# A written order for four engines in the opening of a three-stage kernel: gram copies first, weight conversions spread over more steps

## The chip, the cores and the metric

One Trainium2 chip, one of its cores. The metric is the device time of one execution in microseconds (us), the median of three runs. Engines are called by their short names: PE is TensorE, DVE is VectorE, ACT is ScalarE, POOL is GpSimd, SP is SyncE (here it only issues DMAs). PSUM is the memory that PE writes; SBUF is the working memory.

## The reference, cut to what matters

Three stages follow each other: a delta-rule attention, a dense MLP and a top-1 mixture of experts. Only the first two overlap with the change.

```python
def _attn_ref(q, k, v, beta):            # (4, 8, 768, 48) each, beta (4, 8, 768)
    k_n = k / (np.linalg.norm(k, axis=-1, keepdims=True) + 1e-06)
    state = np.zeros((B, H, D, D)); y = np.zeros_like(q)
    for t in range(S):
        kt, vt, bt = k_n[:, :, t], v[:, :, t], beta[:, :, t, None]
        y[:, :, t] = np.einsum('bhd,bhde->bhe', q[:, :, t], state)
        v_old = np.einsum('bhde,bhd->bhe', state, kt)
        state = state + bt[..., None] * np.einsum('bhd,bhe->bhde', kt, vt - v_old)
    return y

def _moe_ref(x, w_in, w_out):            # x (3072, 384), w_in (384, 2048), w_out (2048, 384)
    h = x @ w_in
    return np.maximum(0.01 * h, h) @ w_out
# then _moe2_ref: each token goes to one of 8 experts (384 -> 1024 -> 384), scaled by two gates
```

## The kernel before

**Attention in chunks.** The 768 tokens are cut into 12 chunks of 64. Within a chunk the recurrence is a triangular solve. For each pair of chunks the kernel needs the gram matrix of the keys (`k_gram`, on PE), copies of its diagonal blocks to `td` and of its off-diagonal ones to `lx` (`k_gram_out`, on ACT and DVE), the norms (`norms`), and the inverse of a 32x32 triangle per head and half chunk (`inverse`: 30 rows, two instructions or more each). The inverse of the first pair (w = 0) runs on DVE and that of every later pair on POOL. Its transpose (`flipped`) goes to `z` through copies (`z_make`).

**The chain.** `chain(k, c)` is a generator. Each `run(ch)` moves chunk c one stage on: clear `ks` and add the values (two DVE instructions), three `solve` groups of small PE matmuls with copies between them (`take`: one half on ACT, one on DVE), the new state, and the outputs `y`, which leave in two float16 parts `xx` (ACT, then DVE) and pass through six small DMAs from SBUF to SBUF (line 395).

**The MLP.** `moe1_up` is one step of eight for a chunk: 18 matmuls to `h` in a `psL` bank, a copy scaled by 0.01 (ACT, `g32`), the maximum (DVE), a float16 copy (ACT, `gh`) and the rest (DVE, `gl`). `moe1_down` is 12 matmuls. Float32 products are made of float16 parts (a high and a low one), so both weights have a high and a low part.

**Weight conversions.** The weights arrive as raw words, 24 pieces of 128x512 (`conv_load`). For each piece `conv` runs three bit operations on DVE into a PSUM tile `wt`, two copies on ACT (`ws`, then the high part) and one subtraction on POOL (the low part, line 468). Step s of the MLP needs the pieces of its own columns only.

**The order.** `weave` first brings pair 0 to its inverse, then runs 16 steps: n = 0 to 7 hold chunk 0's chain and two conversions each, n = 8 to 15 hold chunk 0's MLP, chunk 1's chain and one conversion each. `prepare(1)` spreads the norms and the inverse of pair 1 over them. Up to here the framework sorts each engine's instructions by its own schedule model, with `high_priority` and `issue_after` as hints. From n = 16 on an order written out by hand holds (`manual_schedule`). The file is the same from there in both kernels.

PSUM has eight banks: `psA` 2, `psS` 2, `psL` 2, `psO0` and `psO1`. An `h` tile and a conversion's `wt` can share the two of `psL`.

Of the kernel before, what the change touches and what calls it, by code (L numbers as in the profile page):

```python
# [168 lines left out]
def norms(k, w, td):  # L169
    nc = k.nc  # L170
    V, G = nc.vector, nc.gpsimd
    E = V if w == 0 else G
# [26 lines left out]
    E.tensor_tensor(z, z, z, op=ALU.mult)
    E.tensor_tensor(z, z, k.beta[:, w], op=ALU.mult)  # L200
    E.tensor_scalar(n2, z, -1.0, None, op0=ALU.mult)
    E.tensor_tensor(x, x, n2.unsqueeze(1).to_broadcast([128, 32, 32]), op=ALU.mult)
    if w:
        E.affine_select(x, x, pattern=[[1, 32], [-1, 32]], compare_op=ALU.is_gt, fill=0.0, base=0, channel_multiplier=0)
    E.memset(xf[:, 0:1024:33], 1.0)
    V.transpose(s.nw, y)
    return s
# [63 lines left out]
def q_products(k, c):  # L271
# [4 lines left out]

    def mask():
        for ab in range(2):
            k.nc.vector.tensor_tensor(t.ap[:, GM * ab : GM * ab + GM], gq[ab], k.amask[:, ab : ab + 1].to_broadcast([128, GM, 64]), op=ALU.mult)
# [18 lines left out]
def chain(k, c):  # L298
# [9 lines left out]
    def take(dst, scale):  # L308
        k.mark_uh = A.activation(dst[:, ms[0]], ks[0], AF.Copy, scale=scale)  # L309
        k.mark_u = V.tensor_scalar(dst[:, ms[1]], ks[1], scale, None, op0=ALU.mult)  # L310
# [34 lines left out]
    y = []  # L345
# [16 lines left out]
    with k.tc.issue_after(k.mark_y.ins) if c == 1 else ExitStack():  # L362
        solve(t.z, r, 1, 1, True)
# [4 lines left out]
    if c < NCH - 1:  # L368
        sc, sc_w = spilled(k, k.state[c % 2])
        for m in range(GM):  # L370
            for ab, s in ALL4:
                f = GM * ab + m
                PE.matmul(ks[s][half(ab, 48), m], t.kg[half(s), f], u[half(s), f], start=True, stop=True, skip_group_check=True)
        if c == 0:
# [9 lines left out]
    for m in range(GM):  # L384
        for ab, s in ALL4:
            read(s ^ ab, ab, m, u_w, GM * ab + m, half(s), t.ap, c == 0, True)
    for g in gs:
# [21 lines left out]
def moe1_setup(k):  # L409
    nc, sb = k.nc, k.const  # L410
    V, A, G = nc.vector, nc.scalar, nc.gpsimd
    k.wg = [sb.tile([128, 3, 16], F16, name=f"wg{h}") for h in range(2)]
    wg32 = sb.tile([128, 3, 16], F32, name="wg32")
    nc.sync.dma_start(wg32, k.wg_d.rearrange("p (a e) -> p a e", a=3))
    A.activation(k.wg[0], wg32, AF.Copy, scale=1024.0)
    V.scalar_tensor_tensor(k.wg[1], wg32, 1024.0, k.wg[0], op0=ALU.mult, op1=ALU.subtract)
# [3 lines left out]
    V.tensor_copy(k.cmat, cst)  # L420
# [5 lines left out]
    V.tensor_copy(k.run, k.base)  # L426
# [5 lines left out]
    nc.sync.dma_start(k.xd[DUM : DUM + 1, :], dum)  # L432

# [5 lines left out]
def conv_load(k, pool, n):  # L439
# [4 lines left out]
    else:  # L444
        raw = pool.tile([128, 1024], I32, tag="w64", name=f"w64_{n}")
# [4 lines left out]
def conv(k, pool, n):  # L450
    nc = k.nc
    V, A, G = nc.vector, nc.scalar, nc.gpsimd
    i, which = n // 2, n % 2
    dst, sc = ((k.win, 1024.0), (k.wout, 2048.0))[which]
    w64 = k.w64.pop(n)
    ps, tag = (k.psO, f"psO{n // 2 % 2}") if n < 8 and n % 2 else (k.psL, "psL")
    wt = ps.tile([128, 512], I32, tag=tag, name=f"wt_{n}")
    lo, hi = w64[:, :, 0], w64[:, :, 1]
    V.tensor_scalar(wt, hi, 5, 2, op0=ALU.logical_shift_left, op1=ALU.logical_shift_right)
    V.scalar_tensor_tensor(wt, hi, -0x40000000, wt, op0=ALU.bitwise_and, op1=ALU.bitwise_or)  # L460
    V.scalar_tensor_tensor(wt, lo, 29, wt, op0=ALU.logical_shift_right, op1=ALU.bitwise_or)
    w32 = wt.bitcast(F32)
    cs = slice(512 * i, 512 * i + 512)
    h, l = (columns(d)[:, cs] for d in dst)
    ws = pool.tile([128, 512], F32, tag="wt", name=f"ws_{n}")
    A.activation(ws, w32, AF.Copy, scale=sc)  # L466
    A.activation(h, ws, AF.Copy)
    G.tensor_tensor(l, ws, h, op=ALU.subtract)
# [478 lines left out]
def weave(k):  # L947
    nc = k.nc
    def prepare(w):
        a, b = 2 * w, 2 * w + 1  # L950
        td = k.xp.tile([128, 32, 32], F32, tag="xx", name=f"td{w}")
        yield
        yield
        k_gram(k, a, td)
        yield
        yield
        yield
        k_gram(k, b, td)
        yield
        yield  # L960
        with k.tc.high_priority():
            s = norms(k, w, td)
        yield
        for i in range(6):
            inverse(k, w, s, CUTS[i], CUTS[i + 1])
            if i == 5:
                nv_load(k, a)
            yield
        done = k.after
        with k.tc.issue_after(done.ins):  # L970
            nv_make(k, a, s)
        nv_load(k, b)
        yield
        with k.tc.issue_after(done.ins):
            nv_make(k, b, s)
        with k.tc.issue_after(k.mark_gl.ins) if hasattr(k, "mark_gl") else ExitStack():
            flipped(k, w, s)
        z_make(k, a, s)
        yield
        z_make(k, b, s)  # L980

# [11 lines left out]
    k_load(k, 2)  # L993
    q_load(k, 0)
    nv_load(k, 0)
    es = ExitStack()
    wst = es.enter_context(k.tc.tile_pool(name="wst", bufs=2))
    conv_load(k, wst, 0)
    conv_load(k, wst, 1)
    nconv, nback = 0, 0  # L1000
    td = k.p1.tile([128, 32, 32], F32, tag="td", name="td0")
    for c in range(2):
        ga = gram_banks(k, c)
        for s in range(2):
            gram(k, ga, k.chunks[c].kc, k.chunks[c].kc, ((0, s), (1, s)))
        k_gram_out(k, c, td, ga)
    mark_td = k.mark_td
    s0 = norms(k, 0, td)
    masked_scale(k, s0)
    nv_make(k, 0, s0)  # L1010
    inverse(k, 0, s0, 1, 31)
    moe1_setup(k)
    ch = chain(k, 0)
    run(ch)
    run(ch)
    z_make(k, 0, s0, True)
    after = k.after
    turn = nc.gpsimd.tensor_copy(k.const.tile([128, 1], F32, name="turn"), k.z[0][:, 15, 31:32])

    def convert():  # L1020
        nonlocal nconv, es
        if nconv < 24:
            conv(k, wst, nconv)
            ahead = nconv + (10 if nconv < 2 else 6 if nconv < 12 else 2)
            if (nconv < 2 or nconv >= 6) and not 12 <= nconv < 16 and ahead < 24:
                conv_load(k, wst, ahead)
            nconv += 1
            if nconv == 24:
                es.close()
                k.bg = k.late.enter_context(k.tc.tile_pool(name="bg", bufs=6))  # L1030

    k_load(k, 3)
    kg_load(k, 0)
    nv_load(k, 1)
    for n in range(2, 10):
        conv_load(k, wst, n)
    pg = prepare(1)
    hold = ExitStack()
    for m in (mark_td, turn, after):
        hold.enter_context(k.tc.issue_after(m.ins))  # L1040
    for _ in range(4):
        run(pg)
    q_gram(k, 0)
    run(pg)
    for _ in range(3):
        run(pg)
    up = down = tail = None
    for n in range(16):
        p, s = n // 8, n % 8
        if n:  # L1050
            with k.tc.high_priority() if p == 0 else ExitStack():
                run(ch)
        else:
            nv_make(k, 1, s0)
        if n == 1:
            z_make(k, 1, s0)
        if n == 3:
            hold.close()
            hold.enter_context(k.tc.issue_after(k.mark_u.ins))
            hold.enter_context(k.tc.issue_after(k.mark_uh.ins))  # L1060
        if p < 2:
            for _ in range(2 if p == 0 else 1):
                convert()
        down, up = up, None
        if p >= 1:
            moe1_up(k, p - 1, s)
            up = (p - 1, s, k.gg)
        run(tail)
# [320 lines left out]
```

## Time and profile before

| what | value |
|---|---|
| median of 3 runs | 850.45 us (849.51 to 851.61) |
| the profiled execution | 855.32 us, span 853.4 us |
| PE busy | 768.0 us, 90% of the span |
| DVE busy | 483.4 us, 57% |
| ACT busy | 328.6 us, 39% |
| POOL busy | 414.4 us, 49% |

The span runs from the first instruction to the last; the profiled execution's own time is 1.9 us longer, and 4.9 us above the median of the runs. Busy shares are means over stages with different limits, so they are to be read by stretch. PEclk is the clock that PE was granted, as a share of its full 2.4 GHz.

### The profile page before, as it was taken

What the parts mean: (1) busy time and instruction counts of PE and PEld (TensorE: products, weight loads), DVE (VectorE), ACT (ScalarE), POOL (GpSimd) and SP (SyncE); (2) the same over time, 40 slices, a digit from 0 to 9 for tenths busy, and PEclk for the clock granted to TensorE, in tenths of its full rate; (3) what the DMA queues carried; (4) which work ended last, traced back from release to release, by engine and by line L of the source; (5) the groups of instructions that cost most, each with busy time, mean ns of one, the idle gap of its engine ahead of it and who ended that gap; (6) DMA issues with size and microseconds to landing.
All of it is one profiled execution on the core that took longest, in us unless ns stands there. A gap on an engine that the chain in (4) does not pass through costs nothing. (4 is left out here: it accounts for less than half of the span.)

```text
span 853.4 us, 29444 instructions
## 1 busy us (share of the span) xinstructions
PE 768.0 (90%) x12642; PEld 591.4 (69%) x12642; DVE 483.4 (57%) x1109; ACT 328.6 (39%) x650; POOL 414.4 (49%) x590
## 2 busy tenths in 40 slices
PE   4044898999999999999999999999997999999993
PEld 4044676777777777777777777777775778778782
DVE  2999784766666566657666767775362222222230
ACT  2246546434644464445534465543311111111110
POOL 0017995688468846884588526521132221222110
PEclk7555799999999999999999999999998999999997
DMA  8714434724662458244724397948726537898440
GB/s 265 269 51 148 153 108 142 183 82 142 194 205 71 138 183 228 73 139 144 216 81 139 121 271 214 319 142 323 326 69 221 84 85 214 223 337 232 134 115 13
DMA packets 100137, 145.03 MB, mean 170 GB/s; under 512 B 42320, under 2 KB 69747, under 8 KB 97186
## 3 DMA queue, kind: packets, MB, share of 16 engines
q1 hardware_dynamic: 94882, 128.10, 49.5%
q0 software_dynamic: 5120, 15.00, 5.7%
q8 instruction: 101, 1.65, 0.8%
q14 instruction: 34, 0.28, 0.1%
HBM read 152.28 MB, written 35.42 MB: 220 GB/s over the span
## 5 line engine op out<-in xcount | busy, mean ns | idle before, releaser
L518 PE MATMUL h<-xx,win 128*128 128x256 f16 x1728 | 207.1, 275 | 1.4 <-ACT ws L466 1.4
L543 PE MATMUL o<-wout,gh 128*128 128x384 f16 x768 | 186.0, 326 | 0.7 <-ACT u L309 0.6
L518 PEld LDWEIGHTS <-win 128*128 128x128 f16 x1728 | 164.5, 98 | 27.7 <-issue 1.4
L543 PE MATMUL o<-wout,gl 128*128 128x384 f16 x384 | 123.6, 326 | 2.5 <-DVE gl L532 2.5
L888 PEld LDWEIGHTS <-wb 128*128 128x128 f16 x2016 | 115.7, 98 | 4.8 <-issue 1.4
L528 DVE SCALAR_TENSOR_TENSOR h<-h,g 128x512 f32<-128x512 f32 x96 | 66.7, 695 | 72.1 <-ACT g L525 67.8
L525 ACT ACTIVATE g<-h 128x512 f32<-128x512 f32 x96 | 57.3, 597 | 122.6 <-PE h L518 114.2
L888 PE MATMUL hp<-xT,wb 128*128 128x128 f16 x1728 | 100.9, 220 | 0.0
L892 DVE SCALAR_TENSOR_TENSOR h<-hp,h 128x512 f16<-128x512 f32 x48 | 33.2, 692 | 118.8 <-ACT h L891 108.8
L543 PEld LDWEIGHTS <-gh 128*128 128x128 f16 x768 | 70.8, 98 | 42.7 <-issue 0.8
L491 POOL TENSOR_SCALAR we<-we 128x512 f32<-128x512 f32 x35 | 52.8, 1510 | 97.8 <-ACT whl L487 78.2
L532 DVE TENSOR_TENSOR gl<-h,gh 128x512 f16<-128x512 f32 x96 | 66.3, 690 | 58.1 <-ACT gh L529 56.9
L902 PE MATMUL o<-wb,h 128*128 128x384 f16 x576 | 97.4, 326 | 0.0
L908 POOL DMA_INDIRECT out_dram<-y,row x24 | 23.9, 998 | 141.5 <-DVE y L907 135.5
L529 ACT ACTIVATE gh<-h 128x512 f16<-128x512 f32 x96 | 57.3, 597 | 85.6 <-DVE h L528 85.5
L891 ACT ACTIVATE h<-hp 128x512 f16<-128x512 f32 x48 | 28.7, 597 | 157.8 <-PE hp L888 157.8
L232 POOL TENSOR_TENSOR x<-x,tmp 128x30 f32<-128x30 f32 (+9 forms) x150 | 81.3, 542 | 11.2
L230 POOL TENSOR_TENSOR tmp<-x 128x30 f32<-128x30 f32 (+9 forms) x150 | 77.9, 519 | 10.8
L902 PEld LDWEIGHTS <-h 128*128 128x128 f16 x576 | 55.3, 98 | 34.4
L487 ACT ACTIVATE whl<-we 128x512 f16<-128x512 f32 x96 | 56.6, 623 | 6.8 <-DMA we<-in_we_dram 3.5
L316 PE MATMUL ks<-r,z 32*32 32x48 f32 x1536 | 27.6, 212 | 35.0 <-DVE z L259 28.2
L494 DVE SCALAR_TENSOR_TENSOR whl<-we,whl 128x512 f16<-128x512 f32 x61 | 51.9, 869 | 10.9 <-ACT whl L487 9.2
(253 smaller groups left out, 1018.3 us busy)
## 6 DMA issues: line engine op xcount, KB each, us to landing
wb<-wd SPq DMA_DIRECT2D x56, 1536.0 KB
we<-in_we_dram SPq DMA_DIRECT2D x96, 256.0 KB
wd<-whl SPq DMA_DIRECT2D x96, 256.0 KB
kc<-in_kt_dram SPq DMA_DIRECT2D x24, 224.0 KB
q<-in_qt_dram SPq DMA_DIRECT2D x24, 224.0 KB
nv<-in_kv_dram SPq DMA_DIRECT2D x12, 384.0 KB
kn<-in_kv_dram SPq DMA_DIRECT2D x12, 384.0 KB
w<-in_win_dram SPq DMA_DIRECT2D x6, 512.0 KB
```

The source lines that it names most:

```text
L230: E.tensor_tensor(tv, x[:, q, j : j + 1].to_broadcast([128, n, j]), x[:, j : j + 1, 0:j].to_broadcast([128, n, j]), op=ALU.mult)
L232: k.after = E.tensor_tensor(x[:, q, 0:j], x[:, q, 0:j], tv, op=ALU.add)
L487: nc.scalar.activation(hl[:, 0], w32, AF.Copy, scale=sc)
L491: nc.gpsimd.tensor_scalar(w32, w32, sc, None, op0=ALU.mult)
L518: PE.matmul(hp[:, ff], k.win[l][:, f, kk], xx[:, r, kk], start=(n == 0), stop=(n == 8))
L525: A.activation(g32, hp, AF.Copy, scale=0.01 * 2.0**-10)
L528: V.scalar_tensor_tensor(hp, hp, 2.0**-10, g32, op0=ALU.mult, op1=ALU.max)
L529: k.mark = A.activation(gh, hp, AF.Copy)
L532: k.mark_gl = V.tensor_tensor(gl, hp, gh, op=ALU.subtract)
L543: k.mark_down = k.nc.tensor.matmul(k.o[t], gg[l][:, ff, 128 * t : 128 * t + 128], k.wout[r][:, f], start=(f == 0 and i == 0), stop=(f == N ...
L888: PE.matmul(hp[:, ff], w1[:, l, kk, 128 * f : 128 * f + 128], t.xT[:, 3 * r + kk], start=(i == 0), stop=(i == 8))
L902: nc.tensor.matmul(o, t.h[l][:, f], w2[:, r, f], start=(i == 0), stop=(i == 23))
```

## The change

Up to step 16, PE, DVE, ACT and POOL now keep the order of the program text. The parts:

1. The four copies to `td` of chunks 0 and 1 come first on ACT and DVE, then the four to `lx`, then the norms. The conversions of the small constants (`cmat`, `wg`) follow; they are on ACT, and `gate_weights` waits until the eighth step.
2. The loads are issued in another order; `conv_load` of a later piece follows right behind the conversion that frees its place (`NEXT`).
3. Chunk 2's gram goes to `psL`, chunk 3's to `psO`; both grams and their copies come before the first inverse.
4. `chain` calls `k.fill()` ahead of its copies. For chunk 0 the five fills hold the norms of pair 1, the mask of the first query products, and six conversions.
5. These first six conversions (`EARLY`) use a bank that PE filled before, and get their low part from a PE matmul and an ACT copy; POOL has no part in them. Every conversion's three DVE operations now follow one another, save where two of them stand ahead of the MLP's maximum and the third ahead of `gl`.
6. Seven conversions come before the first MLP step. The other 17 lie in the eight steps: 2, 3, 3, 3, 2, 2, 2, 0.
7. Pair 1's inverse on POOL: rows 1 to 12 behind chunk 0's chain, then three rows a step. `norms` for pair 0 is on DVE as before; pair 1 uses `norms_first` and `norms_second`.

```diff
 def gram_banks(k, c):
-    ps, tags = (k.psO, ("psO0", "psO1")) if c in (1, 2) else (k.psS, ("psS", "psS"))
+    ps, tags = (k.psO, ("psO0", "psO1")) if c in (1, 3) else (k.psL, ("psL", "psL")) if c == 2 else (k.psS, ("psS", "psS"))
...
     def take(dst, scale):
+        k.fill()
         k.mark_uh = A.activation(dst[:, ms[0]], ks[0], AF.Copy, scale=scale)
...
+def conv_bank(k, ps, tag, name):
+    wt = ps.tile([128, 512], I32, tag=tag, name=name)
+    k.nc.tensor.matmul(wt.bitcast(F32), k.ident, k.ident.unsqueeze(1).to_broadcast([128, 4, 128]), start=True, stop=True)
+    return wt
...
+class Conv:
...
+    def vector(self):
...
+        V.tensor_scalar(wt, hi, 5, 2, op0=ALU.logical_shift_left, op1=ALU.logical_shift_right)
+        yield
+        V.scalar_tensor_tensor(wt, hi, -0x40000000, wt, op0=ALU.bitwise_and, op1=ALU.bitwise_or)
+        yield
+        V.scalar_tensor_tensor(wt, lo, 29, wt, op0=ALU.logical_shift_right, op1=ALU.bitwise_or)
+        self.w32 = wt.bitcast(F32)
+        if n in NEXT:
+            conv_load(k, k.wst, NEXT[n])
+    def scalar(self):
+        k, A = self.k, self.k.nc.scalar
+        if self.bank is not None:
+            A.activation(self.h, self.w32, AF.Copy, scale=self.sc)
+        else:
+            ws = k.wst.tile([128, 512], F32, tag="wt", name=f"ws_{self.n}")
+            A.activation(ws, self.w32, AF.Copy, scale=self.sc)
+            A.activation(self.h, ws, AF.Copy)
+            k.nc.gpsimd.tensor_tensor(self.l, ws, self.h, op=ALU.subtract)
+            self.w32 = None
+    def low(self):
+        if self.bank is not None:
+            self.k.nc.tensor.matmul(self.w32, self.k.minus[:, self.n % 2], self.h, start=False, stop=True, skip_group_check=True)
+            self.k.nc.scalar.activation(self.l, self.w32, AF.Copy, scale=self.sc)
...
+    order = es.enter_context(k.tc.manual_schedule(engines={E.PE, E.DVE, E.Activation, E.Pool}))
...
+    for c in range(2):
+        td_out(k, c, td, gas[c])
+    for c in range(2):
+        for ab in range(2):
+            lx_out(k, c, gas[c], ab)
     s0 = norms(k, 0, td)
+    nc.scalar.activation(k.cmat, cst, AF.Copy)
...
+    inverse(k, 0, s0, 1, 31)
     z_make(k, 0, s0, True)
...
+    fills += [
+        [lambda: pair.update({1: norms_first(k, 1, td)}), vec],
+        [mask, vec],
+        [vec, vec],
+        [lambda: norms_second(k, 1, pair[1]), vec],
+        [vec],
+    ]
+    run(ch)
+    sca()
+    run(ch)
+    low()
+    sca()
+    z_make(k, 1, s0)
...
+    inv(12)
+    ch = chain(k, 1)
+    run(ch)
+    low()
+    banks.clear()
+    ops(3)
+    run(ch)
+    sca()
     up = down = tail = None
+    for n in range(8, 16):
+        s = n - 8
         down, up = up, None
+        moe1_up(k, 0, s, (lambda: ops(BEFORE[s]), lambda: ops(1)))
+        up = (0, s, k.gg)
+        sca()
+        inv(1)
+        for _ in range(AFTER[s]):
+            ops(3)
+            sca()
+        if s == 0:
+            q_products(k, 1)()
+        if s < 6:
+            run(ch)
...
+        sca()
+        inv(2)
+        if s == 6:
+            q_products(k, 2)()
         if s == 7:
+            ch = chain(k, 2)
             run(ch)
+            td = k.p1.tile([128, 32, 32], F32, tag="td", name="td2")
+            ga = k_gram(k, 4)
+            k_gram_out(k, 4, td, ga)
+            flipped(k, 1, pair[1])
+            z_make(k, 2, pair[1])
+            z_make(k, 3, pair[1])
...
         if down is not None:
             moe1_down(k, *down)
...
+ORDER = (*range(17), 18, 17, 20, 19, 22, 21, 23)
+NEXT = {0: 10, 1: 11, 6: 12, 7: 13, 8: 14, 9: 15, 2: 16, 10: 17, 11: 18, 16: 19, 18: 20, 17: 21, 20: 22, 19: 23}
+EARLY = 6
+BEFORE = (2, 2, 2, 2, 2, 2, 2, 2)
+HOMES = "010101010SSLLLLLLLAAAALL"
+AFTER = (1, 2, 2, 2, 1, 1, 1, 0)
```

`ops(n)` issues the next n DVE operations of the conversions, `vec()` three of them, `sca()` the ACT and POOL part of those that are complete, `low()` the PE and ACT part of the early six, `inv(n)` the next n rows of pair 1's inverse.

## Rows read from the trace of the kernel before

**Rows 1.** Stretches of the span; the first line names the columns, (x) are counts.

```profile
core 0: us, PE busy (x) PEld busy (x) DVE busy (x) ACT busy (x) POOL busy (x), PEclk, DMA share, GB/s
19.07:50.30 31.23, 2.87 (x82) 2.49 (x79) 30.23 (x143) 5.85 (x14) 1.90 (x1) 0.50 0.59 203
50.30:139.40 89.10, 68.81 (x1340) 53.65 (x1340) 73.38 (x119) 49.92 (x95) 67.54 (x106) 0.76 0.38 128
176.00:600.00 424.00, 420.03 (x7566) 317.58 (x7565) 280.11 (x628) 206.66 (x416) 268.23 (x378) 1.00 0.57 175
```

**Rows 2.** Timeline of ACT, 3 to 20 us: start, duration, instruction, idle before.

```profile
7.16 1.54 ACT L111 ACTIVATE td<-ga 32x256 f32<-32x256 f32 x4 [4.85 <-PE ga L77]
...
15.76 0.24 ACT L415 ACTIVATE wg<-wg 128x48 f16<-128x48 f32 x1 [5.62 <-DMA wg<-in_wg_dram]
15.90 1.52 ACT L111 ACTIVATE td<-ga 32x256 f32<-32x256 f32 x4
```

**Rows 3.** Timeline of DVE, 3 to 20 us.

```profile
7.95 1.76 DVE L109 COPY td<-ga 32x256 f32<-32x256 f32 x4 [7.02 <-ACT td L111]
...
19.07 1.25 DVE L180 STREAM_TRANSPOSE x<-td 128x1024 f32<-128x1024 f32 x1
```

**Rows 4.** Timeline of DVE: the first z copy, and the transpose of pair 1's inverse.

```profile
49.91 0.37 DVE L259 COPY z<-zt 128x256 f32<-128x256 f32 x1
...
138.13 1.25 DVE L241 STREAM_TRANSPOSE zt<-x 128x1024 f32<-128x1024 f32 x1 [5.05 <-POOL x L234]
```

**Rows 5.** Timeline of PE: grams 0 and 1, first solve, MLP steps n = 8 and 17.

```profile
3.82 5.38 PE L77 MATMUL ga<-kc 48*64 48x64 f32 x128 [3.82 <-DMA kc<-in_kt_dram]
...
50.34 2.47 PE L316 MATMUL ks<-r,z 32*32 32x48 f32 x64 [28.23 <-DVE z L259]
...
91.76 4.00 PE L518 MATMUL h<-xx,win 128*128 128x256 f16 x18 [1.41 <-ACT ws L466]
...
143.79 2.14 PE L518 MATMUL h<-xx,win 128*128 128x256 f16 x18
```

**Rows 6.** Timeline of DVE: two operations of one conversion, then two unrelated ones.

```profile
93.13 0.70 DVE L459 TENSOR_SCALAR wt<-w 128x512 int32<-128x512 int32 x1 [0.89 <-ACT ws L466]
93.86 0.70 DVE L460 SCALAR_TENSOR_TENSOR wt<-w,wt 128x512 int32<-128x512 int32 x1
...
99.25 0.69 DVE L459 TENSOR_SCALAR wt<-w 128x512 int32<-128x512 int32 x1
99.85 0.69 DVE L528 SCALAR_TENSOR_TENSOR h<-h,g 128x512 f32<-128x512 f32 x1
```

**Rows 7.** DVE's groups by shape, 50.3 to 139.4 us: busy, mean ns of one.

```profile
L279 DVE TENSOR_TENSOR ap<-gq,amask 128x512 f32<-128x512 f32 x6 | 4.0, 680 | 0.0
L332 DVE SCALAR_TENSOR_TENSOR ks<-nv,nw 128x384 f32<-128x384 f32 x4 | 3.2, 826 | 0.0
L390 DVE SCALAR_TENSOR_TENSOR xx<-y,xx 112x512 f16<-112x512 f32 x4 | 2.7, 684 | 0.0
L310 DVE TENSOR_SCALAR u<-ks 128x384 f32<-128x384 f32 x4 | 2.2, 549 | 1.0 <-PE ks L316 1.0
```

**Rows 8.** The page's costliest groups: an ACT copy of 128x512.

```profile
L525 ACT ACTIVATE g<-h 128x512 f32<-128x512 f32 x96 | 57.3, 597 | 122.6 <-PE h L518 114.2
```

**Rows 9.** Timelines of SP's queue and PE: xx DMAs of chunks 0 and 11; chunk 11's first h.

```profile
79.24 4.79 SPq L395 DMA_DIRECT2D xx<-xx  x6
...
562.37 3.90 SPq L395 DMA_DIRECT2D xx<-xx  x6
...
570.69 2.13 PE L518 MATMUL h<-xx,win 128*128 128x256 f16 x18
```

**Rows 10.** Three stretches of 4 us, columns as in the first group.

```profile
80.00:84.00 4.00, 3.40 (x94) 3.21 (x90) 4.00 (x10) 1.35 (x3) 2.69 (x7) 0.50 0.28 85
92.00:96.00 4.00, 4.00 (x34) 2.60 (x32) 2.33 (x4) 2.20 (x4) 3.84 (x8) 0.50 0.38 139
136.00:140.00 4.00, 1.72 (x15) 1.20 (x13) 1.87 (x3) 0.87 (x2) 2.02 (x2) 1.00 0.94 321
```

More of the change, by code (lines that the diff above doesn't have):

```diff
@@ L361, in chain @@
         state_part(gs)
-    with k.tc.issue_after(k.mark_y.ins) if c == 1 else ExitStack():
-        solve(t.z, r, 1, 1, True)
+    solve(t.z, r, 1, 1, True)
     if c > 1:
@@ L444, in conv_load @@
     else:
-        raw = pool.tile([128, 1024], I32, tag="w64", name=f"w64_{n}")
+        raw = pool.tile([128, 1024], I32, tag="w64", bufs=3, name=f"w64_{n}")
     k.nc.sync.dma_start(raw, (k.win_d, k.wout_d)[which][i].bitcast(I32))
     k.w64[n] = raw.rearrange("p (a b) -> p a b", b=2)
[L450 to L468, printed above, removed]
@@ L948, in weave @@
     nc = k.nc
[L949 to L980, printed above, removed]
     def run(g):
@@ new lines, in weave, with fill, stream @@
+    q_load(k, 1)
+    for n in range(6, 10):
+        conv_load(k, k.wst, n)
+    kg_load(k, 1)
+    nback = 0
+    E = mybir.EngineType
+    order = es.enter_context(k.tc.manual_schedule(engines={E.PE, E.DVE, E.Activation, E.Pool}))
+    ready, fills = [], []
+    def fill():
+        for f in fills.pop(0) if fills else ():
+            f()
+    k.fill = fill
+    def stream():
+        homes = dict(zip("01SLA", ((k.psO, "psO0"), (k.psO, "psO1"), (k.psS, "psS"), (k.psL, "psL"), (k.psA, "psA"))))
+        for n, home in zip(ORDER, HOMES):
+            u = Conv(k, n, banks[n % 4] if n < EARLY else None, homes[home])
+            for _ in u.vector():
+                yield
+            ready.append(u)
+            yield
@@ L1001, in weave, with ops, vec, inv @@
+    late = []
+    todo = stream()
+    def ops(n):
+        for _ in range(n):
+            next(todo, None)
+    def vec():
+        ops(3)
+    rows = iter(range(1, 31))
+    def inv(n):
+        for j in [j for _, j in zip(range(n), rows)]:
+            inverse(k, 1, pair[1], j, j + 1)
+    def sca():
+        for u in ready:
+            u.scalar()
+            late.append(u)
+        ready.clear()
+    def low():
+        for u in late:
+            u.low()
+        late.clear()
     td = k.p1.tile([128, 32, 32], F32, tag="td", name="td0")
+    gas = []
@@ L1015, in weave @@
     run(ch)
-    z_make(k, 0, s0, True)
[L1017 to L1046, printed above, removed]
-    up = down = tail = None
[L1048 to L1063, printed above, removed]
-        down, up = up, None
[L1065 to L1068, printed above, removed]
-        if s == (5 if p == 0 else 4):
-            q_load(k, p + 1)
+    mask = q_products(k, 0)
@@ new lines, in weave @@
+    ga = k_gram(k, 3)
+    k_gram_out(k, 3, td, ga)
+    banks = [conv_bank(k, k.psO, f"psO{i}", f"wb{i}") for i in range(2)] + [conv_bank(k, k.psL, "psL", f"wc{i}") for i in range(2)]
+    inverse(k, 0, s0, 1, 31)
+    z_make(k, 0, s0, True)
+    nc.gpsimd.tensor_copy(k.const.tile([128, 1], F32, name="turn"), k.z[0][:, 15, 31:32])
+    pair = {}
+    fills += [
[5 more added lines that the diff above has]
+    ]
@@ L1082, in weave @@
+            z_make(k, 2, pair[1])
+            z_make(k, 3, pair[1])
+        if s == 1:
+            k_load(k, 4)
+        if s in (2, 3):
+            nv_load(k, s)
+            nv_make(k, s, pair[1])
+        if s == 3:
+            q_load(k, 2)
+        if s == 5:
+            kg_load(k, 2)
+        if s == 6:
+            gate_weights(k, wg32)
         if down is not None:
             moe1_down(k, *down)
-            if down[1] == 7:
-                tail = moe1_tail(k, down[0], k.o)
-        with k.tc.issue_after(k.mark_down.ins) if down is not None else ExitStack():
-            if n and n not in (1, 3, 15):
-                run(pg)
-            if n == 12:
-                td = k.p1.tile([128, 32, 32], F32, tag="td", name="td2")
-            if n == 13:
-                k_load(k, 5)
```

136 lines of the change are left out of this document (81 added, 55 removed).

## The prediction

> **What bounds the kernel now.** I read the stretches first. From 176 to 600 us PE is busy 420.0 of 424.0 us at full clock [rows 1]: there PE is the bound, its work is the same in both kernels, and whatever is won or lost before it arrives whole at the end. So the question is only when step 17 starts; its first MLP matmul stands at 143.79 us [rows 5]. PE saturates from about there.
>
> Before that DVE is the bound, in two stretches. From the norms (19.07) to the first z (50.3) it is busy 30.23 of 31.23 us while PE waits 28.2 us for that z [rows 1, 4, 5]. From z to the transpose of pair 1's inverse it has 73.4 us of work in 89.1 us [rows 1]; PE in the same stretch has 68.8 us busy at a mean clock of 0.76, so PE is slow because it waits. That transpose ends at 138.13 + 1.25 = 139.38 us, after 5.05 us of waiting for POOL [rows 4]. The z copies of chunks 2 and 3 follow on ACT, then the solve that opens step 17.
>
> One more place costs time: the timeline of ACT shows chunk 0's td copies at 7.16, but chunk 1's only at 15.90, because the small wg conversion stood ahead of them and waited 5.62 us for its DMA [rows 2]. DVE's norms wait for these copies.
>
> **First stretch: the gram copies.** With td first, ACT takes chunk 1's copies right after chunk 0's (7.16 + 1.54 + 1.54 = 10.2 us). DVE does its own first four from 7.95 to 9.71 and the next four, of the same 1.76, to 11.47 [rows 3]. PE has both grams done at 3.82 + 5.38 = 9.2 us [rows 5], before DVE's second four and ACT's last ones need them. So the norms start at 11.5 instead of 19.07 [rows 3], 7.6 us earlier. From there to z DVE has the same instructions, 31.2 us [rows 1], so z is ready at 42.7 us. The constants now convert behind the copies on ACT. They are needed when the values go into ks, after the norms (a transpose of 1.25 [rows 3] and some 22 small instructions of about 0.2, the mean of that stretch [rows 1]: not before 17 us). So they cost nothing if their DMAs land early, and nothing at 15.76 either, where wg landed before [rows 2]. ACT is busy 5.85 of 31.23 us there [rows 1], which hides the added copies of chunks 2 and 3.
>
> **From z to pair 1's transpose.** I walk DVE in order; t is time since z. A conversion's operations, one after another, start 0.73 us apart (93.13, 93.86), unrelated operations 0.60 (99.25, 99.85) [rows 6]: a conversion that stands alone takes 0.73 + 0.73 + 0.60 = 2.06 us.
>
> Chunk 0's five stages. Each is a fill and then DVE's half of the copies (0.55) [rows 7]; the solves of 2.47 us on PE [rows 5] lie under fills. Stage 1: transpose 1.25 [rows 3], three small operations of about 0.2 (the mean of the 143 instructions of the first stretch [rows 1]), a conversion, the copy: t = 4.5. Stage 2: two masks at 0.60 [rows 6, 7], a conversion, the copy: 8.3. Stage 3: two conversions, the copy: 12.9. Stage 4: two small operations, a conversion, the state copy: 16.0. Stage 5: a conversion to 18.0, then ACT's xx copy of 0.60 [rows 8] and DVE's two of 0.69 [rows 7]: 19.4. In the kernel before the xx DMAs go out at 79.24 - 50.3 = 28.9 [rows 9].
>
> The six DMAs take 4.79 us to issue. How long the last takes to land no row shows. Below: nothing. Above: chunk 11's end at 566.27 and its first matmul at 570.69 does not wait, 4.4 us [rows 9]. I take the middle, 2.2: xx is there at t = 26.4. (The Trainium skill, DMA: Bandwidth & Descriptors, section Anatomy of one DMA, gives about 2.0 us of fixed cost; by it the sum would be 0.2 us shorter, which no run here shows.) The first h then takes 4.00 us at the low clock [rows 5] and ACT's copy 0.60: t = 31.0. Meanwhile DVE does chunk 1's values (2 x 0.83), the seventh conversion, a copy of 0.55 [rows 7] and two conversion operations, to 25.1. It then idles 5.9 us. This stall is new: in the kernel before more conversions covered it.
>
> The eight steps. Maximum, third operation and gl, with gl waiting for ACT, take 2.05 us, or 3.35 with the two operations in front. Step 0: 2.05, a conversion, two masks, a copy: 36.8. Step 1: 3.35 + 2 x 2.06 + 0.55 = 8.0, to 44.8. Step 2 the same and 0.5 of waiting, since the next g32 stands on ACT behind two conversions' copies: 53.3. Step 3: 3.35, two conversions, two state additions, 0.5 of the same wait: 62.4. Step 4: 3.35, one conversion, then 1.9 for ACT to come free for xx, and 1.3: 70.9. Step 5: 5.3, to 76.2. Step 6: 5.4, two masks, 0.4 for the gate weights, 0.7 of waiting: 83.9. Step 7: 2.2, values of chunk 2 1.4, transpose 1.25: 88.75.
>
> So the transpose ends at 42.7 + 88.75 = 131.45 us against 139.38: 7.9 earlier, of which 7.6 come from the first stretch. The second stretch stays as long as it was (88.75 against 89.1): its 5 us wait for POOL goes, and 5.9 us for xx and the dependent pairs come. POOL would be ready in time: 67.5 us of work before [rows 1], less six subtractions, spread over t = 2 to 82. Queued behind POOL's rows are the subtractions, and behind these the two `ws` buffers of ACT; by my walk it trails DVE by 1 to 2 us.
>
> Of the 7.9 I take off 0.5: chunk 4's copies now stand on ACT ahead of z, and PE has one h and one `moe1_down` left before the solve. Sum: 143.79 becomes 136.3, a gain of 7.4 us. The profiled execution took 855.32, so 847.9 by it; it lies 4.9 us above the median of the runs, and from that median the same gain gives 850.45 - 7.4 = **843.0 us**. What a measurement tells from no change is 0.3%, 2.6 us.
>
> **Rivals.**
> *The second stretch is shorter too.* If the DVE operations of a conversion follow at 0.60 (33 pairs x 0.13 = 4.3 us) and xx lands at once (2.2), 6.5 us more are gained: 836.5. For it: before, DVE was kept 99% busy by interleaving. Against: dependent pairs at 0.73 stand in the trace [rows 6].
>
> *PE's clock falls for a while.* In steps 1 to 4 PE has about 5.5 us of work at full clock in 8 to 9 us: an h of 2.14, a down of as many columns (12 x 384 = 18 x 256), and a chain stage, half of the 2.47 that a solve took at the low clock [rows 5]. Pauses of some 2.5 us lie behind ACT's late copies. The kernel before held the full clock through 136 to 140 us with 1.72 of 4 us busy, but was at half clock with 3.40 busy at 80 to 84 [rows 10]: both happen. From low clock, 92 to 96 us was spent fully busy before it rose [rows 10]. A fall makes a step 10.5 (4.00 + 4.00 + 2.47), some 2 us above DVE's pace, until it rises again; one to three falls cost 2 to 5 us: 845 to 848. The Trainium skill (TensorE: Matmul & The Clock Gate, section HAM oscillation) speaks for it: bursts of matmuls with pauses between them fall back to the low clock each time. The stretch at 136 us, though with one long pause only, goes against it.
>
> *The other side: the low clock holds through all eight steps.* Then PE is the bound with 10.5 us a step. 42.7 + 26.4 + 8 x 10.5 = 153.1, and about 4 (one more h) to step 17: 157.1, 13.3 us later than before: 864. It ends slower from 8.8 us a step on ((143.79 - 42.7 - 26.4 - 4) / 8), that is when some two thirds of PE's work runs at half clock. Against: full activity raised it in the kernel before within 4 to 5 us.
>
> *The conversions moved behind chunk 0 eat the gain.* POOL's queue decides: if its rows or subtractions run late, ACT waits for a `ws` buffer, then DVE for the PSUM tile. By my walk its rows end 7 us before DVE wants them, so POOL would have to take some 15 us more than its 67.5 before [rows 1] to undo the 7.4; the result is then about 850. Its 67.5 us are those of 89.1, so it is unlikely.
>
> **Numbers.** My forecast 0.50, with its own range 839 to 847; shorter second stretch 0.22; clock falling for a while 0.12; low clock throughout 0.08; no net change through POOL 0.08. Faster by over 0.3% are the first two and most of the third, 0.83; within it 0.09; slower 0.08. The range reaches down past the second case, 835 for the uncertain landing, and up to 849 for the third and the edge of the fourth.
>
> **What would show it.** Right: norms at about 11.5 and z at about 42.7 us; xx DMAs at about 62; a DVE gap of 4 to 8 us before the first maximum; steps 1 to 3 of 8 to 9 us; pair 1's transpose near 131 and no wait for POOL there; step 17's h near 136; no difference in length after it. Wrong: chunk 1's td copies still late; the granted clock at 0.50 between 75 and 125 us; ACT or DVE waiting for POOL's subtractions; SP holding xx behind a weight load.

## The result, and the profile after

| | before | after |
|---|---|---|
| median of 4 runs, same chip | 849.98 us (847.31 to 851.61) | 840.34 us (838.73 to 841.61) |
| ratio to before, 95% interval | | 0.9889 [0.9858, 0.992] |
| profiled execution, its span | 855.32, 853.4 us | 840.49, 838.5 us |

The change made the kernel 9.6 us faster; 7.4 were predicted (840.3 us against a forecast of 843.0). The stretches of after, cut at the same events as [rows 1] (columns as there):

```profile
core 0: us, PE busy (x) PEld busy (x) DVE busy (x) ACT busy (x) POOL busy (x), PEclk, DMA share, GB/s
12.57:44.01 31.44, 6.31 (x134) 4.14 (x134) 30.35 (x143) 10.22 (x28) 1.44 (x1) 1.00 0.87 290
44.01:130.54 86.53, 64.00 (x1262) 45.29 (x1262) 74.47 (x121) 47.34 (x86) 61.43 (x100) 0.88 0.36 119
...
176.00:600.00 424.00, 423.25 (x7576) 319.47 (x7575) 277.76 (x627) 210.85 (x424) 261.02 (x365) 1.00 0.59 185
```

The first stretch begins at 12.57 instead of 19.07 and is as long as before (31.44 against 31.23 us): it was moved, not shortened. The second is 2.6 us shorter (86.53 against 89.10), with 1.1 us more DVE work in it. The timeline of ACT at the start, to be read beside [rows 2]:

```profile
7.08 1.54 ACT L110 ACTIVATE td<-ga 32x256 f32<-32x256 f32 x4 [4.77 <-PE ga L77]
9.98 1.54 ACT L110 ACTIVATE td<-ga 32x256 f32<-32x256 f32 x4 [1.35 <-PE ga L77]
...
12.85 0.52 ACT L1069 ACTIVATE cmat<-cmat 128x384 f16<-128x384 f32 x1
13.26 0.23 ACT L1070 ACTIVATE wg<-wg 128x48 f16<-128x48 f32 x1
```

Chunk 1's copies stand where the `wg` conversion waited 5.62 us, and `wg`, loaded earlier and converted later, waits for nothing. The timeline of DVE, beside [rows 3, 4]:

```profile
7.88 1.76 DVE L108 COPY td<-ga 32x256 f32<-32x256 f32 x4 [6.94 <-ACT td L110]
10.77 1.76 DVE L108 COPY td<-ga 32x256 f32<-32x256 f32 x4 [1.13 <-ACT td L110]
12.57 1.25 DVE L181 STREAM_TRANSPOSE x<-td 128x1024 f32<-128x1024 f32 x1
...
43.63 0.38 DVE L253 COPY z<-zt 128x256 f32<-128x256 f32 x1
...
71.76 0.70 DVE L560 SCALAR_TENSOR_TENSOR h<-h,g 128x512 f32<-128x512 f32 x1 [3.90 <-ACT g L557]
...
129.30 1.24 DVE L235 STREAM_TRANSPOSE zt<-x 128x1024 f32<-128x1024 f32 x1
```

Pair 1's transpose no longer waits for POOL; the wait of 3.90 us ahead of the first maximum (71.76) is new. SP's queue, then PE's MLP matmuls and, last, the solve and the MLP matmul that open step 17 (in two fences), beside [rows 5, 9]:

```profile
63.10 4.00 SPq L401 DMA_DIRECT2D xx<-xx  x6
```

```profile
65.83 0.82 PE L550 MATMUL h<-xx,win 128*128 128x256 f16 x3 [0.59 <-DMA xx<-xx]
67.13 0.82 PE L550 MATMUL h<-xx,win 128*128 128x256 f16 x3 [0.48 <-DMA xx<-xx]
68.35 2.74 PE L550 MATMUL h<-xx,win 128*128 128x256 f16 x12 [0.40 <-DMA xx<-xx]
...
92.99 2.13 PE L550 MATMUL h<-xx,win 128*128 128x256 f16 x18 [2.44 <-ACT ws L491]
...
101.47 2.96 PE L550 MATMUL h<-xx,win 128*128 128x256 f16 x18 [2.39 <-ACT ws L491]
...
121.71 4.02 PE L550 MATMUL h<-xx,win 128*128 128x256 f16 x18 [4.19 <-DVE gl L564]
...
134.61 0.88 PE L321 MATMUL ks<-r,z 32*32 32x48 f32 x64
135.43 2.14 PE L550 MATMUL h<-xx,win 128*128 128x256 f16 x18
```

The first h does not wait for the last of the six DMAs: it begins 2.7 us after the first was issued and does six of its 18 matmuls as parts arrive. Step 17's h stands at 135.43 against 143.79, 8.36 us earlier.

What releases step 17 has changed too. In the kernel before, the solve ahead of its h waits for ACT's copy `r`, which stands behind the z copies and so behind pair 1's transpose:

```profile
142.97 0.88 PE L316 MATMUL ks<-r,z 32*32 32x48 f32 x64 [1.17 <-ACT r L309]
```

In after the same solve, at 134.61, waits for nothing. ACT is done with `r` at 133.70, 0.9 us before PE comes to it, and PE has worked without a gap since 121.71. So what sets step 17 there is the `gl` of step 6, for which PE waited 4.19 us, and the 13.7 us of PE's work behind it; pair 1's transpose has a little time to spare.

### The profile page after: what moved, and what is told of

Read it like the earlier page. It is cut to its first block, busy times and chain, and to the rows that moved or that the text cites. A ratio compares the mean times of both kernels' runs of the same rounds, so it can differ in the third digit from the quotient of the medians.

```text
span 838.5 us, 29440 instructions
## 1 busy us (share of the span) xinstructions
PE 765.2 (91%) x12652; PEld 586.0 (70%) x12652; DVE 482.5 (58%) x1108; ACT 330.0 (39%) x653; POOL 408.8 (49%) x584
## 5 line engine op out<-in xcount | busy, mean ns | idle before, releaser
L550 PE MATMUL h<-xx,win 128*128 128x256 f16 x1728 | 210.1, 277 | 10.5 <-ACT ws L491 4.8
L575 PEld LDWEIGHTS <-gl 128*128 128x128 f16 x384 | 37.5, 98 | 25.9 <-DVE gl L564 1.3
```

Of the source, the lines that this page charges most:

```text
L550: PE.matmul(hp[:, ff], k.win[l][:, f, kk], xx[:, r, kk], start=(n == 0), stop=(n == 8))
L575: k.mark_down = k.nc.tensor.matmul(k.o[t], gg[l][:, ff, 128 * t : 128 * t + 128], k.wout[r][:, f], start=(f == 0 and i == 0), stop=(f == N ...
```

## The experiments

The table has four blocks: the first pair, e1 to e4, a1 to e8, and e3c to a2. Kernels of one block ran on one chip, which also ran the kernel before; ratios are to that chip's before. "zt" is the start of pair 1's transpose, "h17" step 17's first MLP matmul, all starts in us in the profiled execution. Of kernels that were profiled unchanged on several chips, h17 differs by up to 1.3 us (before) and 1.0 us (after); differences of that size between two profiles show nothing.

| run | norms | z | zt | h17 | median, runs | ratio [95%] |
|---|---|---|---|---|---|---|
| before (first pair) | 19.07 | 49.91 | 138.13 | 143.79 | 849.98, 4 | |
| after (first pair) | 12.57 | 43.63 | 129.30 | 135.43 | 840.34, 4 | 0.9889 [0.9858, 0.992] |
| e1, before again | 19.34 | 50.19 | 138.45 | 145.08 | 859.06, 1 | |
| e2, `wg` first again | 19.84 | 50.92 | 136.94 | 142.99 | 856.91, 10 | 1.0002 [0.9984, 1.002] |
| e3, copies before conversions | 16.87 | 47.71 | 136.03 | 142.66 | 855.60, 10 | 0.9973 [0.9956, 0.9989] |
| e4, ten operations out | 11.24 | 42.32 | 122.58 | 128.72 | 842.47, 4 | 0.9837 [0.9811, 0.9862] |
| a1, after again | 12.08 | 43.16 | 129.12 | 135.17 | 839.88, 4 | 0.9888 [0.9861, 0.9914] |
| e3b | 19.34 | 50.69 | 138.99 | 144.96 | 850.31, 10 | 1.0003 [0.9985, 1.002] |
| e5, one unit earlier | 11.81 | 42.88 | 128.87 | 134.92 | 839.54, 4 | 0.9886 [0.9846, 0.9927] |
| e8, last two homes | 12.21 | 43.28 | 128.71 | 135.82 | 839.08, 4 | 0.9879 [0.9859, 0.9899] |
| e3c, copies and norms first | 12.55 | 43.92 | 132.33 | 138.28 | 850.32, 6 | 0.9912 [0.9891, 0.9933] |
| e12, eight rows, one unit | 12.05 | 43.13 | 128.30 | 132.88 | 846.93, 4 | 0.9877 [0.9862, 0.9891] |
| e13, and one home | 12.31 | 43.39 | 128.98 | 133.57 | 847.09, 4 | 0.9874 [0.9859, 0.9888] |
| a2, after again | 11.80 | 42.88 | 128.35 | 134.40 | 849.60, 5 | 0.9913 [0.99, 0.9925] |

Medians of before beside the three later blocks: 857.41, 849.89 and 857.55 us.

The theory is the prediction's: DVE sets the pace up to step 17, the gain comes from the gram copies and is carried to the end. The rivals: the gain needs the new order behind z; or something else (POOL, PE, the part after step 17) makes it.

**e1: is the later part faster too?** Behind h17 the first two profiles differ by another 6.5 us (709.6 against 703.1), and that was not predicted. Edit: none.

> The kernel before, unchanged, profiled once more. From step 17's first MLP matmul to the span's end the first profile of before took 709.6 us and the profile of after 703.1 us, and PE of before pauses some 0.4 us at a time with no wait that the profile shows. Theory: these pauses belong to that one execution; here the stretch takes 703 to 705 us, step 17's matmul stands again near 143.5, the profiled execution takes about 850. Rival: the change itself shortens the part after step 17 by 6.5 us; then the stretch takes about 709 us again, with the pauses at the same steps.

The rival's number came: 857.1 - 145.08 = 712.0 us, with the pauses. But on that chip every profile had them, that of the new weave too (h17 to the end of the span: e2 711.4, e4 711.1).

**a1: after on another chip.** Edit: none.

> The kernel after, unchanged, on the chip of the runs beside it. In the first pair of profiles the part behind step 17's first MLP matmul took 703.1 us in after and 709.6 in before; in the four runs since then, all with PE pauses of some 0.4 us near 229, 317, 405 and 540 us, it took about 711, whatever was changed. Theory: the later part belongs to the chip or the execution; here after shows those pauses and about 710 us for that part too, and the ratio to before is again 0.989. Rival: after does shorten the later part by 6 us; then no pauses, about 704 us, whatever before takes.

Here no pauses at those places and 702.4 us; but e3b, the old weave on the same chip, has none there either and takes 704.6. On the chip of the last block e3c takes 711.5 and after itself (a2) 711.0. The places, from the timelines of PE in before's first profile and in a2:

```profile
229.16 0.57 PE L77 MATMUL ga<-kc 48*64 48x64 f32 x19 [0.39 <-issue]
233.01 0.43 PE L316 MATMUL ks<-r,z 32*32 32x48 f32 x18 [0.44 <-issue]
```

```profile
219.18 0.53 PE L77 MATMUL ga<-kc 48*64 48x64 f32 x18 [0.38 <-issue]
223.25 0.42 PE L321 MATMUL ks<-r,z 32*32 32x48 f32 x16 [0.47 <-issue]
```

So this part follows the chip or the execution. Cut at the MLP's last h matmul it is plainer still: from h17 to there it takes 457.7 us in the first profile of before and 451.2 in that of after, which is the whole 6.5 us; it takes 455.9 to 457.1 in the eight later profiles that have the pauses, and 451.6 to 452.9 in the four of the chip of a1, old weave (e3b, 451.6) and new (a1, 451.6) alike. Behind that matmul e3b takes 2.3 to 4.5 us more than the three of the new weave beside it, while the first pair is equal there (251.9 us); why stays open. Below, medians and ratios are compared on one chip only. Starts ahead of step 17 are also compared across chips, as not every chip has a profile of both kernels.

**e2: undo the first part in after.** The constants are loaded behind q, v and two weights again, chunk 3's k behind them, and `wg` is converted ahead of chunk 1's copies.

```
-    nv_load(k, 0)
-    wg32, cst = moe1_loads(k)
...
-    k_load(k, 3)
+    nv_load(k, 0)
...
+    wg32, cst = moe1_loads(k)
+    k_load(k, 3)
...
+        if c == 1:
+            nc.scalar.activation(k.wg[0], wg32, AF.Copy, scale=1024.0)
         td_out(k, c, td, gas[c])
```

> The kernel after with one part undone: the conversion of wg stands on ACT ahead of chunk 1's td copies again, and its DMA is issued where the kernel before issued it, behind chunk 0's q and v and the first two weights. Theory (DVE is the bound up to z): norms start near 19 instead of 12.57 and everything to step 17 moves by the same 6.3 us; step 17's matmul at about 141.7, the time about 846.7. Rival: the wait is hidden later, because the stretch after z is held by transfers and POOL rather than by its start; then step 17's matmul moves by less than 3 us and the time stays below 843.

The timeline of ACT:

```profile
17.00 0.24 ACT L1065 ACTIVATE wg<-wg 128x48 f16<-128x48 f32 x1 [8.27 <-DMA wg<-in_wg_dram]
17.25 1.54 ACT L110 ACTIVATE td<-ga 32x256 f32<-32x256 f32 x4
```

Norms and h17 move together (7.27 and 7.56 us against the first profile of after, which is from another chip) and the kernel is as slow as before. The wait is not hidden anywhere later. What is left of the change, all of the new order behind z, shows as 2.1 us at h17 against e1 and as nothing in the time (0.5 us, interval -1.4 to +1.7), where the theory's 846.7 left some 3.8 us of gain.

**e3, e3b, e3c: the first part alone, in before.** Three edits; only the third does what was meant. e3 puts the conversion of `wg` on ACT behind ACT's last td copy, and those of `wg`, `cmat` and `run` on DVE behind DVE's last; e3b puts all four behind the norms; e3c puts ACT's behind the last td copy and DVE's three behind the norms. The core of e3c:

```
+    with k.tc.issue_after(k.mark_td.ins):
         A.activation(k.wg[0], wg32, AF.Copy, scale=1024.0)
+    with k.tc.issue_after(k.mark_n.ins):
         V.scalar_tensor_tensor(k.wg[1], wg32, 1024.0, k.wg[0], op0=ALU.mult, op1=ALU.subtract)
```

> The kernel before with one part of the change alone: the conversions of wg, of the constant matrices and of run are put behind the td copies of chunks 0 and 1, the loads keep their order. Theory: norms start at 12 to 13 instead of 19.07, z 6 us earlier, step 17's matmul at about 137.5, the time about 844. Rival: the gain needs the written order of the weave behind it as well, since pair 1's transpose waited 5.05 us for POOL; if POOL's end is set by something else than z, the norms start early but step 17's matmul stays at 141 to 143 and the time at 848 to 850.

> The kernel before with the gram copies first and nothing else: the conversions of wg, of the constant matrices and of run wait until the norms are done (in the run before this one they came first on DVE, which waited 3.74 us for wg). Theory: norms at about 12.5 instead of 19.1 to 19.3, z at about 43.5, and pair 1's transpose and step 17's matmul come by the same 6 us earlier: 138.5 to 139, a ratio of 0.992 to 0.993. Rival (POOL, for which the transpose waited 5 to 6 us, ends when its own work and loads allow): less than half of it arrives, ratio above 0.996.

> The kernel before with the gram copies first on both engines: ACT's conversion of wg stands behind chunk 1's td copies, DVE's conversions of wg, the constant matrices and run stand behind the norms. Theory: norms at 12 to 12.6 instead of 19.1 to 19.3, z and all that follows 6.5 to 7.5 us earlier, so step 17's matmul near 137 to 138 and a ratio of 0.991 to 0.993; the rest of the gain of after (9.8 us at that matmul) is then 2 to 3 us and belongs to the stretch behind z. Rival: the start is early but DVE or POOL lose it again before step 17; ratio above 0.996.

In the kernel before, DVE's queue had the same wait as ACT's, which [rows 2, 3] and the prediction do not show: its own `wg` operation stood ahead of its copies for chunk 1, which came at 17.27.

```profile
16.03 0.21 DVE L416 SCALAR_TENSOR_TENSOR wg<-wg,wg 128x48 f16<-128x48 f32 x1 [6.32 <-ACT wg L415]
```

In e3 ACT's copies are free of it, and on DVE it stands behind the copies but still ahead of the norms; the timeline of DVE:

```profile
16.01 0.21 DVE L418 SCALAR_TENSOR_TENSOR wg<-wg,wg 128x48 f16<-128x48 f32 x1 [3.74 <-ACT wg L416]
16.52 0.36 DVE L423 CAST cmat<-cmat 128x384 f16<-128x384 f32 x1 [0.30 <-DMA cmat<-in_cmat_dram]
16.80 0.17 DVE L430 COPY run<-crow 128x8 f32<-128x8 f32 x1
16.87 1.24 DVE L180 STREAM_TRANSPOSE x<-td 128x1024 f32<-128x1024 f32 x1
```

The norms came 2.5 us earlier and so did everything else, h17 2.4 and the median 1.8 (ratio 2.3). In e3b the edit did not do what it says: ACT's conversion stayed ahead of the copies,

```profile
16.61 0.24 ACT L416 ACTIVATE wg<-wg 128x48 f16<-128x48 f32 x1 [6.58 <-DMA wg<-in_wg_dram]
16.76 1.52 ACT L111 ACTIVATE td<-ga 32x256 f32<-32x256 f32 x4
```

so it tells nothing of its theory; it is a second reading of before. In e3c the copies do come first, and the timeline of DVE shows

```profile
12.55 1.25 DVE L180 STREAM_TRANSPOSE x<-td 128x1024 f32<-128x1024 f32 x1
...
132.33 1.25 DVE L241 STREAM_TRANSPOSE zt<-x 128x1024 f32<-128x1024 f32 x1 [5.59 <-POOL x L234]
```

z stands 6.3 us earlier than in e1, zt 6.1, h17 6.8 (against the first profile of before: 6.0, 5.8 and 5.5), and the ratio is 0.9912: 7.5 us. POOL's end, for which zt waits as in [rows 4], moves with z and is no fixed time. The rival falls. Beside e3c, a2 is at h17 3.9 us earlier still (1.0 of it from z, 2.8 from the stretch behind), but the medians differ by 0.7 us only, with runs from 847.62 to 853.03 and 847.48 to 851.03.

**e4: is DVE the bound behind z?**

```
-        V.scalar_tensor_tensor(wt, hi, -0x40000000, wt, ...)
+        if n not in (8, 10, 11, 13, 14, 16, 18, 20, 22, 23):
+            V.scalar_tensor_tensor(wt, hi, -0x40000000, wt, ...)
```

> The kernel after with the second of the three bit operations of ten weight conversions left out (units 8, 10, 11, 13, 14, 16, 18, 20, 22 and 23, which stand between chunk 1 and step 7; the sign bits of these weights are then missing). It takes ten operations of 0.60 to 0.73 us from DVE. Theory (DVE is the bound from z to pair 1's transpose): that transpose, at 129.30 in the kernel after, and step 17's matmul, at 135.43, come 5 to 7 us earlier, the time is about 834 to 835. Rival (PE's matmuls with ACT's copies, or POOL's subtractions, set the pace of the eight steps): they come less than 2 us earlier, and the time is 838.5 to 840.

From z to h17 it takes 86.40 us against 91.80 in the first profile of after, 92.01 in a1 and 91.52 in a2: 5.1 to 5.6 us, of the 6.0 to 7.3 us taken from DVE. The ratio is 0.9837 against 0.9888 and 0.9913 for after. DVE sets most of the pace there, as forecast. Up to about 1 us of it may be PE's: step 4's h took 2.12 us here, against 2.96 and 3.75 in the first profile of after and in a1, and ACT had waited 0.32 and 1.11 us for those.

**e5: one conversion more under the first stall.**

```
     ops(3)
     run(ch)
     sca()
+    ops(3)
+    sca()
...
-AFTER = (1, 2, 2, 2, 1, 1, 1, 0)
+AFTER = (0, 2, 2, 2, 1, 1, 1, 0)
```

> The kernel after with unit 7 converted ahead of step 0 instead of after it, into the 3.9 us in which DVE waits for the first h. Theory that DVE alone sets the pace: one conversion of 2.06 us less on its path, pair 1's transpose and step 17's matmul 1.5 to 2 us earlier, ratio to after about 0.998. Rival (POOL): ACT waited 3.15 us at unit 8 for a subtraction queued behind twelve rows of POOL; that wait stays, and less than 0.5 us arrives.

It went the rival's way. ACT's timeline, first of a1 and then of e5 (unit 8, then the g of step 1):

```profile
76.88 0.60 ACT L491 ACTIVATE ws<-wt 128x512 f32<-128x512 f32 x1 [3.15 <-POOL win L493]
...
78.41 0.59 ACT L557 ACTIVATE g<-h 128x512 f32<-128x512 f32 x1
```

```profile
76.88 0.60 ACT L491 ACTIVATE ws<-wt 128x512 f32<-128x512 f32 x1 [4.77 <-POOL win L493]
...
78.42 0.59 ACT L557 ACTIVATE g<-h 128x512 f32<-128x512 f32 x1
```

ACT's copy of unit 8 starts at the same 76.88 us in both, though z is 0.28 us earlier and a conversion less stands in front: the wait grew by 1.6 us instead. It waits for a `ws` buffer, whose subtraction stands on POOL behind twelve rows of the inverse.

**e12: and POOL's rows.** As e5, and:

```
-    inv(12)
+    inv(8)
```

> The kernel after with unit 7 converted ahead of step 0, which alone brought nothing, and with eight rows of POOL's inverse instead of twelve ahead of its first subtraction (the other four follow later). Theory: POOL's queue is what took the gain away; without it ACT's copy of unit 8 no longer waits and the whole conversion arrives, step 17's matmul 1.7 to 2.2 us earlier than in after, ratio to after about 0.9977. Rival: the rows then come late at the end, pair 1's transpose waits for POOL and nothing arrives.

Both came. The wait at unit 8 is gone, and the g of step 1 is at 75.54 against 78.32 in a2 (3.0 us earlier, from z). Then 1.2 us are lost at step 4, whose h took 3.71 us here and 2.13 in a2. And the rival shows, in the timeline of DVE and then of PE:

```profile
128.30 1.25 DVE L235 STREAM_TRANSPOSE zt<-x 128x1024 f32<-128x1024 f32 x1 [2.12 <-POOL x L228]
```

```profile
132.07 0.88 PE L321 MATMUL ks<-r,z 32*32 32x48 f32 x64 [0.68 <-ACT r L311]
```

The solve of step 17 waits for ACT's `r` again, as in the kernel before: now POOL, through the transpose, sets the end of the stretch. From z to h17 1.8 us remain. The median is 846.93 (846.38 to 847.18) against 849.60 (847.48 to 851.03) for after beside it: a little faster than both kernels.

**e8, e13: the pause ahead of step 7.** The first line is after's, the second e8's, the third e13's, which has the edits of e12 as well.

```
-HOMES = "010101010SSLLLLLLLAAAALL"
+HOMES = "010101010SSLLLLLLLAAAAAA"
+HOMES = "010101010SSLLLLLLLAAAAAL"
```

> The kernel after with the PSUM tiles of the last two weight conversions in psA instead of psL, so that step 7's h needn't wait for them: in after PE paused 4.19 us for gl of step 6 ahead of that h, and the h then took 4.02 us instead of 2.14. Theory: the pause and the low clock behind it set the end of the stretch; step 17's matmul comes 1.2 to 2 us earlier. Rival: DVE sets it, which has the same work; less than 0.5 us.

> The run before it with one more edit: the PSUM tile of the last weight conversion but one is in psA instead of psL, so that step 7's h finds a free tile before gl of step 6 while the ks tile behind it still finds one too (with both of the last two in psA, ks waited 2.50 us and nothing was won). Theory: the 4.2 us pause of PE shrinks to 1 to 2 us, step 7's maximum comes 0.5 to 1 us earlier, step 17's matmul 2.3 to 3 us earlier than in after, ratio to after about 0.9968. Rival: h waits for ACT and POOL to finish its weights, PE falls to the low clock all the same, and it is within 0.5 us of the run before.

PE's timeline in e8:

```profile
117.58 0.82 PE L550 MATMUL h<-xx,win 128*128 128x256 f16 x6
119.36 0.39 PE L550 MATMUL h<-xx,win 128*128 128x256 f16 x2 [0.97 <-ACT win L492]
120.59 1.27 PE L550 MATMUL h<-xx,win 128*128 128x256 f16 x10 [0.84 <-POOL win L493]
121.86 0.32 PE L332 MATMUL ks<-cmat 128*128 128x384 f16 x1
124.68 0.32 PE L332 MATMUL ks<-cmat 128*128 128x384 f16 x1 [2.50 <-ACT ws L491]
```

h starts 4.3 us earlier, waits for its weights, and the `ks` matmul behind it waits 2.50 us for the tile that the conversion now holds: zt comes 0.4 us earlier than in a1, h17 0.65 later, and the ratio (0.9879) is after's (0.9888). In e13 the edit did not remove the wait (step 7's h, at 119.64, still waits 4.19 us for gl), and nothing was won over e12 (0.9874 against 0.9877).

**a2.** 

> The kernel after, unchanged, beside the two that are to be compared with it: the ratio to before again 0.989, step 17's matmul at about 135.2.

The ratio is 0.9913 [0.99, 0.9925], near the edge of the others' intervals; h17 is at 134.40. On this chip after gains no more than e3c (0.9912), which has the first part alone.

## Why the prediction was right, step by step

**The bound, and that a shift of the start arrives whole: shown.** e2, e3 and e3c move the norms by 7.3, 2.5 and 6.8 us and h17 by 7.6, 2.4 and 6.8; in the time, e2 loses the whole gain, e3 has 2.3 us of it and e3c 7.5. What is won behind z is not shown to arrive: 2.1 us at h17 in e2 are 0.5 in the median, and the 3.9 us of a2 ahead of e3c are 0.7.

**How near the sum came, and why.** The transpose was forecast to end at 131.45 and ended at 130.54, step 17's h was forecast at 136.3 and came at 135.43. That is nearer than the terms were: the first stretch ended 1.3 us later than forecast (44.01 against 42.7), the second was 2.2 us shorter, and the two errors partly cancel. That much is luck. Of the 2.2 us by which the gain was too small (9.6 against 7.4), 0.9 stand at h17; the profiles, which differ by several us behind it for other reasons, do not resolve the rest.

**First stretch, 7.6 us: too much by up to one.** The norms start at 12.57 (11.24 in e4, which has the same opening, and 11.80 to 12.31 in the six others), not 11.5; z came 6.3 us earlier in the first pair and 7.5 in a1 against e3b. The term that failed is "DVE does ... the next four ... to 11.47": ACT's second four wait for PE until 9.98 instead of starting at 8.7 (by the prediction's own row the grams are done at 9.2 only), and DVE's start 0.79 us behind ACT's, as chunk 0's do in [rows 2, 3] (7.95 against 7.16). The walk let DVE run on. In e4 PE was done sooner, ACT's second four started at 8.65, and DVE did run on.

**Second stretch, 88.75 us: 2.2 us too long.** It took 86.53. The stall for xx was priced at 5.9 us and took 3.9. Three things made the difference: the issue took 4.00, not 4.79; the last part was there 68.35 - 67.10 = 1.25 us behind the end of the issue, not 2.2; and h had a third of its matmuls done by then. The walk had h start when the last part is there. So the first maximum stood 27.75 us behind z, not 31.0. One addition in the walk is off: stage 5 names ACT's copy of 0.60 and DVE's two of 0.69 behind 18.0, which makes 20.0 and not 19.4. It did no harm, as all but 0.26 us of that copy lay under the conversion and the issue began 19.1 us behind z. The Trainium skill (DMA: Bandwidth & Descriptors, section Anatomy of one DMA) gives about 2.0 us of fixed cost, which it states for another issue path than SP's; here that is longer than the 1.25 us of the last part.

One of these 3.25 us was lost again: from the first maximum to the transpose's end it took 58.8 us, 57.75 in the walk. "By my walk it trails DVE by 1 to 2 us" failed for POOL: ACT waited 3.15 us at unit 8, and the maximum of step 1 came 0.79 us late for it. e5 and e12 show that this wait, not DVE's work, fixed the time of step 1. The other terms held: 1.9 us for ACT ahead of xx in step 4 (measured 1.87), conversions 0.73 apart, and 4.85 us from the transpose's end to h17 (measured 4.89). The last held in its number only: the forecast lets step 17 follow from the transpose, with 0.5 us off for what PE has left, and in after it is PE's work that step 17 follows from.

**Where the 5 us wait for POOL went.** It is gone in after: POOL ends its inverse at 123.57, 5.7 us before DVE wants it. e3c shows that its removal was worth little by itself: with the wait still there, 5.59 us, the time is within 0.7 us of after's. How much of the 9.6 us the new order behind z brings stays open: 2 to 3 us at h17 in the profiles, 0 to 1 us in the medians (0.5 by e2, 0.7 by a2 beside e3c).

**Rivals.** *The shorter second stretch* came in one half. Dependent pairs at 0.60 us: not so, they follow at 0.73 as before (64.04 and 64.77 in a1). The early xx: yes, with the 3.25 us above.

*The falling clock* came in part. After's rows show it behind two of PE's pauses (columns as above):

```profile
93.00:95.00 2.00, 2.00 (x18) 1.65 (x17) 1.73 (x3) 1.20 (x2) 1.66 (x2) 1.00 0.00 0
101.50:104.40 2.90, 2.90 (x22) 2.01 (x21) 2.83 (x6) 1.81 (x3) 1.58 (x3) 0.69 0.68 227
121.80:125.70 3.90, 3.90 (x19) 2.75 (x20) 3.29 (x7) 1.67 (x3) 3.38 (x3) 0.50 0.00 0
```

Behind a pause of 2.39 us the granted clock was 0.69 and the h took 2.96 us; behind one of 4.19 it was 0.50 and the h took 4.02; behind one of 2.44 it was 1.00 and the h took 2.13. In a1 the h behind the 2.39 us took 3.75, 0.8 longer, and step 4's g came 0.8 later. ACT waited 0.32 and 0.65 us for the two slow h's in after, 1.11 and 0.29 in a1: up to about 1 us each, not 2 to 5 together. The second h, 1.9 us longer than one at the full clock, also lies in PE's unbroken work ahead of step 17; without it 0.9 us would be won there (an estimate: 134.61 - 133.70), as the transpose is the bound again from then on. The Trainium skill (TensorE: Matmul & The Clock Gate, section HAM oscillation) has bursts of matmuls with waits between them fall back each time; the trace agrees for the pause of 4.18 to 4.20 us, in each of the seven profiles that have it (an h of 3.47 to 4.02 us behind it). The waits in its example are longer than 2.4 us, so the two shorter pauses neither bear it out nor contradict it.

*Low throughout*, and *no net gain through POOL*: neither came (the granted clock from 75 to 125 us was 0.88).

**The part behind step 17.** "No difference in length after it" holds within 1.2 us on the chips of e1 and of a2. On that of a1 it holds up to the MLP's last h, and behind it the one profile of the old weave is 2.3 to 4.5 us longer. The first pair of profiles differs by 6.5 us, all of it ahead of that h, and goes with pauses that e1 to e4 and a2 show to belong to the chip or the execution.

## What to carry to other kernels

A small instruction that waits for a late DMA costs what stands behind it in its engine's queue; look for it on the engines that are not the bound, and when it is moved, look at the queue that it is moved to (e3 lost two thirds of the gain to the same wait on DVE). Where the bound engine feeds a saturated one, time won at the start arrived whole here, so a shift of the first event predicts the end better than a count of the waits removed. A freed gap is only worth filling once the next queue behind it (here POOL's) is shown to be free too: e5 brought nothing, and e12, with four rows of POOL's moved back, 1.8 us at step 17, until POOL's later end set the transpose.

## What the runs showed of the hardware that was not expected

The same kernel before took 849.9 us on one chip (850.0 in the first comparison) and 857.4 to 857.6 on two others, with PE pauses of mostly 0.2 to 0.5 us, put down to "issue", near the same steps of every profile there. The cause stays open. In the first stretch of after PE's granted clock was 1.00 in one profile and 0.51 in another (a1), and from the norms to z both took 31.1 us.
